# Two layers of hedgehog linear attention and squared-ReLU dense block: the join between dense layer and next keys, and the barrier at each layer's start, issued in another order

## The chip, the cores and the metric

One core of a Trainium2 chip runs the whole kernel. The metric is the device time of one execution in microseconds (us), and of the runs shown the median counts. The engines are TensorE (PE in the profile, its weight loads PEld), VectorE (DVE), ScalarE (ACT), GpSimd (POOL) and SyncE (SP, which issues most of the DMA transfers). Each engine works off its own queue in order.

## The reference

Input x has 2048 rows (S) of 576 features (D); there are 32 heads of 18 features and 4608 hidden features. Two layers, each with the same weights, are computed in float32:

```
x = x + A(layernorm(x));  x = x + B(layernorm(x))          # twice
A:  q, k, v = x @ wqkv
    phi(q) = [softmax(q @ w_phi), softmax(-q @ w_phi)]      # per head
    kv = phi(k)^T v ;  z = sum over rows of phi(k)
    o  = phi(q) kv / (phi(q) z + 1e-6) ;  return o @ wo
B:  return relu(x @ w1 + b1)^2 @ w2 + b2
```

Each layer's `kv` and `z` are sums over all rows, so no row can leave layer 1's attention before the last row has left layer 0's dense block.

## The kernel before

**Tiling.** Rows are cut into 4 blocks of 512 (`NB`), each of 4 tiles of 128 (`NT`). Features are held transposed in 5 chunks (four of 128 and a rest of 64), hidden features in 36 chunks `f` of 128 (`NF`). To keep float32 accuracy, each operand of a product is split into a high part that PE reads exactly and a low part that holds the rest, and a product is made of three: high by high, low by high, high by low. The split costs a copy (ACT) and a subtraction (DVE or POOL).

**Order.** A generator traces each stage's instructions; `weave` runs two of them against each other at a given rate, `pipeline` steps tiles through stages, and each `yield` gives the cost of the step. `chained` and `held` put what is traced behind the last instruction of each engine so that the scheduler, which builds the final queue of every engine, can't move it ahead. The blocks are taken as [3, 2, 0, 1]. Blocks 3 and 2 have a dense block each, 0 and 1 share one (`g_pair`): `products` does the first product of both and the second product of block 0, and `seconds` then does the second product of block 1, one `f` after the other, with 12 matmuls of 448 columns and 3 of 512 for each `f`. For a coming `f`, one SP transfer brings the weights (`m_pr`), another the squared activations (`m_pg`), and ACT, DVE and POOL split them into `m_ps` (L1190 to L1192) and `m_phc` (L1276).

**The join.** In layer 0, `seconds` is woven with `back_keys`, which makes layer 1's keys and values of blocks 3, 2 and 0 while PE still works on the dense chunks. For each block it norms four tiles (`n_3`, `n_2`, `n_0`), transposes them on PE in six steps (two pairs of tiles, and behind each pair its rests), splits the result (L412, L413), projects values (`v_3pv`, weights `w_3v0`, `w_3v1` for the two halves of the heads) and keys (`k_3kp`, weights `w_3k0`, `w_3k1`), turns keys into features (the `k_3K` tiles) and adds a tile's share to the sums `kvp`. The value and key weights take turns in the same buffers, and half 0 of the keys needs the buffer that half 0 of the values leaves. A tile's norm is mean and variance on DVE (L375, L376), a power on POOL (`n_2d`, L378) and two scalings on DVE (L393, L394). Block 0 has its keys alone here. Products and transposes share two PSUM buffers (`w`), so a third group can start on PE only when the first has been split.

**The barrier.** At the start of each layer (names `t0` and `t1`) the last blocks' values and sums are finished, the sums are turned into operands (`sums_operands`: `zb`, `ko`, `kbh`, `kbl`, and for the last four heads `kq` with the products `kt`, in `last_group`), and one block's query features are divided by their sums. This is `g_phi`: for tile t, two products `t0fm` (half on DVE, half on POOL), two sums and a few small steps on DVE, and the scaling of the features `t0fQ` by `t0fQr` (half on DVE, half on POOL). `g_out` then transposes the scaled features (L768, `t0opt`), multiplies them by the operands (`t0opn`) and by the output weights (`t0oo0`, `t0oo1`), first for tiles 0 and 1 (part 0) and then for tiles 2 and 3. In layer 0 the output weights are split here, with the low parts on POOL (L331); layer 1 loads the kept parts.

Of the kernel before, what the change touches and what calls it, by code (L numbers as in the profile page):

```python
# [7 lines left out]
F32 = mybir.dt.float32  # L8
# [5 lines left out]
P = 128  # L14
TB = 512
# [6 lines left out]
def layers_kernel(  # L22
# [322 lines left out]

    def moved(which, half, pair, back):
        for piece, home in zip(pair, wsplit[which]):
            for p, c0, c1 in parts_of(which):
                at = half * NC * HP
                here = piece[p, c0:c1].rearrange("p c n -> p (c n)").bitcast(F32)  # L350
                there = home[p, at + c0 * HP : at + c1 * HP]
                nc.sync.dma_start(*((there, here) if back else (here, there)))
# [28 lines left out]
    def g_norm(x_of, dst, name, then=None, fine=False):  # L381
# [3 lines left out]

        def scale(t):
            x = x_of(t)
            mv, rstd = moments(x, t, name)
            if fine:
# [50 lines left out]
        if not fine:  # L440
            yield from lagged(NT, scale, turn_all)
            return
        xns, pts = {}, {}

        def apart(t):
            xns[t] = scale(t)

# [38 lines left out]

    def make_v(x, t, pair, name):
        vt = vslots[dense["v"] % NT]
        dense["v"] += 1
        v3 = vt[:, : H * VW].rearrange("p (h d) -> p h d", d=VW)  # L490
        for half in range(2):
            pt = project(x, t, pair[half], f"{name}pv{half}{t}")
            dense["evicted"] = nc.scalar.activation(v3[:, half * H // 2 : (half + 1) * H // 2, 1:],
                                                    pt[:, :HP].rearrange("p (h d) -> p h d", d=DH), AF.Copy)
        return vt
# [83 lines left out]
    def sums_operands(layer):  # L579
# [22 lines left out]
        def keep(own, parts):  # L602
            hi, lo = parts
            nc.scalar.activation(hi, own, AF.Copy)
            nc.vector.tensor_sub(lo, own, hi.bitcast(F32))


        for s in range(2):
            pt = wtile(f"kt{layer}{s}")
# [11 lines left out]
        def last_group():  # L621
            w = gw[last]
            own = sb.tile([P, TB], F32, tag="hr", name=f"kq{layer}", bufs=2)
            own = own[:, : 2 * w].rearrange("p (s q f) -> p s q f", s=2, q=NQ)
            nc.vector.tensor_mul(own, kv[:, :, HG].unsqueeze(2).to_broadcast([P, 2, NQ, DH]),
                                 quarter.unsqueeze(1).unsqueeze(3).to_broadcast([P, 2, NQ, DH]))
            pt = wtile(f"kt{layer}2")
            p3 = pt[:w, : 2 * w].rearrange("p (s n) -> p s n", s=2)
            with tc.issue_after(dense["projected"].ins):
                for s in range(2):  # L630
                    nc.tensor.matmul(p3[:, s], own[:, s].rearrange("p q f -> p (q f)"),
                                     place.rearrange("p q d -> p (q d)"), start=True, stop=True)
            keep(p3, [k[:w, :, last, :w] for k in (kbh, kbl)])
# [75 lines left out]
    def phi_scale(e, r):  # L709
        for s in range(2):  # L710
            e3 = e[:, s].rearrange("p (h d) -> p h d", d=DH)
            (nc.gpsimd if s else nc.vector).tensor_mul(
                e3, e3, r[:, s].unsqueeze(2).to_broadcast([P, H, DH]))
# [29 lines left out]
    def g_out(layer, b, ph, dst, name, parts=1, pause=None, behind=None, norm=None, mid=None, costs=(None, None)):  # L743
# [377 lines left out]
    def g_pair(layer, blocks, x, after, name):  # L1121
# [217 lines left out]
        def seconds():  # L1339
# [21 lines left out]
    def g_attend(layer, b, x, raws, dst, name, behind=None, norm=None, mid=(None, None), ph=None):  # L1361
# [8 lines left out]
        if mid[0]:  # L1370
            yield from mid[0]
        yield from g_out(layer, b, ph, dst, name, behind=behind and behind["last"], norm=norm, mid=mid[1],
                         costs=(1.0, None if norm else 3.0))
# [10 lines left out]
    def barrier(layer, b, prev, x, xprev, kes, vpair):  # L1384
# [39 lines left out]
        drain(softs)  # L1424
        last_group = sums_operands(layer)
        spare["tags"] = [f"acc{i}" for i in range(NC)] + ["h"]
        phi = g_phi(layer, er, ph, f"{n}f")
        for _ in range(4):
            next(phi)
            next(queries)  # L1430
            next(queries, None)
        drain(queries)
# [38 lines left out]
    for layer in range(2):  # L1471
# [24 lines left out]
        def back_keys():  # L1496
            new_slots("vs")
            late = []
            for b in order[:3]:
                m = f"1_{b}"  # L1500
                last = b == order[2]
                xk, vts, raws, es, rs = {}, [], {}, {}, {}
                yield from g_norm(rows_of(b), xk, f"n{m}", fine=True)
                while late:
                    kv_tile(1, *late.pop(0))
                    yield 0.8
                if not last:
                    spill(b, xk)
                    yield from paced(g_v(xk, wpair("v", f"w{m}"), vts, f"v{m}"), 1.0)
                pair = wpair("k", f"w{m}")  # L1510

                def raw(t):
                    raws[t] = make_raw(xk, t, pair, f"k{m}k")

# [66 lines left out]
```

## Time and profile before

| what | value |
|---|---|
| runs | 2531.08, 2533.43, 2536.16 us (median 2533.43) |
| profiled execution | 2538.57 us, of which the span from first to last instruction is 2536.8 |
| mean granted PE clock | 0.992 |
| PE busy | 2481.7 us, 98% of the span |
| join and dense work around it, 1170 to 1345 us | PE busy 159.51 of 175 us, clock 0.95, DMA share 0.62 |
| barrier of layer 0, 195 to 250 us | PE busy 45.10 of 55 us, clock 0.94 |
| barrier of layer 1, 1455 to 1505 us | PE busy 45.08 of 50 us, clock 0.97 |

The last three rows are windows of the trace. An engine's row in the list of waits reads: the instruction that waited and its line, the instruction that it waited for and its line, the sum of the waits in us, how many, and the longest. A window reads: busy time of PE, PEld, DVE, ACT and POOL, then the granted clock of PE as a share of full speed, the share of DMA engines busy, and GB/s. A row of a timeline reads: start, duration, engine, line, operation, output and inputs, shapes, and in brackets the idle time ahead of it with what ended it.

### The profile page before, as it was taken

Reading aid. Unit: us, or ns where it says so; the run is one execution under the profiler, and the core shown is the slowest. Engines: PE = TensorE matmul, PEld = TensorE weight load, DVE = VectorE, ACT = ScalarE, POOL = GpSimd, SP = SyncE. Lnnn points to the kernel's source line nnn. Section 1 sums busy time; section 2 is a strip of 40 time slices with the busy share of each in tenths; the row PEclk is TensorE's granted clock in tenths of the full one; section 3 lists DMA queues with packets and bytes.
Section 4 is the critical chain, followed back from the end, with each engine's and each line's share of the span. In section 5 each row is a group of like instructions: output and inputs, shape, how many; then the busy total and the mean of one; then the engine's idle time right before and its main releaser. Section 6 shows DMA issues by size and latency. Waiting matters only on the chain.

```text
span 2536.8 us, 41468 instructions
## 1 busy us (share of the span) xinstructions
PE 2481.7 (98%) x15108; PEld 2179.8 (86%) x15108; DVE 1570.9 (62%) x2514; ACT 1265.5 (50%) x2245; POOL 949.5 (37%) x1101
## 2 busy tenths in 40 slices
PE   8998999999999999999999989999999999999999
PEld 8997888889888888888889988888898888888888
DVE  6778848554856655554667679394548566555444
ACT  4344545443446666663333435454445466666642
POOL 3544312212325555551333333031123355565322
PEclk8999999999999999999999999999999999999999
DMA  9222643356434433328654134333563444333363
GB/s 326 79 69 91 196 116 85 103 164 213 133 119 125 143 114 99 113 93 295 206 180 148 47 128 150 102 99 98 166 222 112 129 130 142 116 96 109 112 199 127
DMA packets 249691, 348.52 MB, mean 137 GB/s; under 512 B 30158, under 2 KB 157262, under 8 KB 246926
## 3 DMA queue, kind: packets, MB, share of 16 engines
q1 hardware_dynamic: 248228, 343.18, 42.7%
q8 instruction: 118, 1.93, 0.3%
q10 hardware_dynamic: 1258, 2.70, 0.3%
q14 instruction: 87, 0.71, 0.1%
HBM read 279.46 MB, written 66.32 MB: 136 GB/s over the span
## 4 chain that ended last, share of the span: by engine, by line
PE 47%; DVE 3%; DMA 2%; ACT 1%; POOL 1%; issue 1%; SPq 0%; DVEq 0%; ACTq 0%; POOLq 0%
PE m_1ph L887 5%; PE m_0ph L887 4%; PE m_pacacc L1231 4%; PE m_ppx L1202 4%; PE m_1acc L914 3%; PE m_0acc L914 3%; PE m_pacc L1231 3%; PE m_ppy L1202 2%; PE m_pacacc L1221 2%; PE m_pach L1231 1%; PE m_0acc L905 1%; PE m_1acc L905 1%; PE m_pacc L1221 1%; PE m_ppz L1202 1%; PE a_0po L805 1%
## 5 line engine op out<-in xcount | busy, mean ns | idle before, releaser
L1192 POOL TENSOR_TENSOR m_ps<-m_pr,m_ps 128x128 fp32r<-128x128 f32 x144 | 118.2, 821 | 338.6 <-ACT m_ps L1190 282.9
L1191 DVE TENSOR_TENSOR m_ps<-m_pr,m_ps 128x448 fp32r<-128x448 f32 x144 | 98.1, 681 | 194.7 <-ACT m_ps L1190 191.3
L1231 PE MATMUL m_pacc<-m_ps,m_phb 128*128 128x448 f32 x864 | 188.5, 366 | 0.0
L1231 PEld LDWEIGHTS m_pacc<-m_ps,m_phb 128*128 128x128 f32 x864 | 162.2, 188 | 18.0
L1190 ACT ACTIVATE m_ps<-m_pr 128x576 fp32r<-128x576 f32 x144 | 98.1, 681 | 154.5 <-issue 88.2
L1231 PE MATMUL m_pacacc<-m_ps,m_phc 128*128 128x448 f32 x648 | 147.7, 370 | 0.0
L1231 PEld LDWEIGHTS m_pacacc<-m_ps,m_phc 128*128 128x128 f32 x648 | 122.6, 190 | 9.9
L1212 DVE TENSOR_TENSOR m_phb<-m_pz,m_phb 128x512 fp32r<-128x512 f32 x72 | 56.5, 784 | 113.1 <-ACT m_pz L1211 111.6
L914 PE MATMUL m_2acc<-m_2s,m_2hb 128*128 128x448 f32 x432 | 100.2, 366 | 0.0
L914 PE MATMUL m_0acc<-m_0s,m_0hb 128*128 128x448 f32 x432 | 100.1, 366 | 0.0
L887 PE MATMUL m_3ph<-t0onh,m_3h 128*128 128x512 f32 (+1 forms) x380 | 98.0, 383 | 1.6 <-DVE t0onh L426 0.8
L914 PE MATMUL m_1acc<-m_1s,m_1hb 128*128 128x448 f32 x432 | 99.4, 365 | 0.0
L914 PE MATMUL m_3acc<-m_3s,m_3hb 128*128 128x448 f32 x432 | 99.4, 365 | 0.0
L887 PE MATMUL m_1ph<-t1onh,m_1h 128*128 128x512 f32 (+1 forms) x380 | 97.8, 382 | 1.5 <-DVE t1onh L426 0.8
L887 PE MATMUL m_0ph<-a_0nh,m_0h 128*128 128x512 f32 (+1 forms) x380 | 97.8, 384 | 0.0
L887 PE MATMUL m_2ph<-a_2nh,m_2h 128*128 128x512 f32 (+1 forms) x380 | 97.8, 384 | 0.0
L914 PEld LDWEIGHTS m_2acc<-m_2s,m_2hb 128*128 128x128 f32 x432 | 80.9, 188 | 10.5 <-ACT m_2hb L895 0.2
L914 PEld LDWEIGHTS m_0acc<-m_0s,m_0hb 128*128 128x128 f32 x432 | 80.9, 188 | 10.6 <-ACT m_0hb L895 0.2
L914 PEld LDWEIGHTS m_1acc<-m_1s,m_1hb 128*128 128x128 f32 x432 | 81.1, 188 | 10.3
L914 PEld LDWEIGHTS m_3acc<-m_3s,m_3hb 128*128 128x128 f32 x432 | 81.1, 188 | 10.3
L872 POOL TENSOR_TENSOR m_3s<-m_3r,m_3s 128x128 fp32r<-128x128 f32 x36 | 24.6, 683 | 168.6 <-ACT m_3s L867 154.1
L872 POOL TENSOR_TENSOR m_1s<-m_1r,m_1s 128x128 fp32r<-128x128 f32 x36 | 24.7, 686 | 167.7 <-ACT m_1s L867 153.3
(2440 smaller groups left out, 7372.1 us busy)
## 6 DMA issues: line engine op xcount, KB each, us to landing
m_pr<-in_B_w SPq DMA_DIRECT2D x144, 288.0 KB
m_pr<-in_B_w SPq DMA_DIRECT2D x72, 256.0 KB
hd<-m_pu SPq DMA_DIRECT2D x72, 256.0 KB
m_pg<-hd SPq DMA_DIRECT2D x72, 256.0 KB
m_3r<-in_B_w SPq DMA_DIRECT2D x36, 288.0 KB
m_2r<-in_B_w SPq DMA_DIRECT2D x36, 288.0 KB
m_1r<-in_B_w SPq DMA_DIRECT2D x36, 288.0 KB
m_0r<-in_B_w SPq DMA_DIRECT2D x36, 288.0 KB
```

Of the source, the lines that this page charges most:

```text
L805: nc.tensor.matmul(pt[:, :HP], a, m[:w, g], start=(g == 0 and k == 0), stop=(g == NG - 1 and k == 2))
L872: nc.gpsimd.tensor_sub(s2[:, D + R : 2 * D], r2[:, R:], s2[:, R:D].bitcast(F32))
L887: dense["hidden"] = nc.tensor.matmul(ph[:, cols], a, m, start=(k == 0), stop=(k == len(ops) - 1))
L905: nc.tensor.matmul(acc[KC], a, m, start=(f == 0 and k == 0), stop=(f == NF - 1 and k == 2))
L914: nc.tensor.matmul(acc[t][:, :R], a[:, rows], m, start=(f == 0 and k == 0), stop=(f == NF - 1 and k == 2))
L1190: nc.scalar.activation(s2[:, :D], r2, AF.Copy)
L1191: nc.vector.tensor_sub(s2[:, D : D + R], r2[:, :R], s2[:, :R].bitcast(F32))
L1192: nc.gpsimd.tensor_sub(s2[:, D + R : 2 * D], r2[:, R:], s2[:, R:D].bitcast(F32))
L1202: nc.tensor.matmul(ps, a, m, start=start and i == 0, stop=i == len(ms) - 1, skip_group_check=True)
L1212: nc.vector.tensor_sub(hl, r, hh.bitcast(F32))
L1221: nc.tensor.matmul(accs[b][KC], a, m, start=(g == 0 and k == 0), stop=(g == NF - 1 and k == 2))
L1231: nc.tensor.matmul(accs[b][t][:, :R], a[:, rows], m, start=(g == 0 and k == 0), stop=(g == NF - 1 and k == 2))
```

## The change

Part 1 is the join. `chained` gets a strict form which also puts each step of `back_keys` behind PE's last traced instruction. `seconds` yields five times in each `f` instead of once, and the rate goes from 4.0 to 0.85; six instead of two steps are taken within the last paired product. The norm is cut into statistics and scaling, pipelined over tiles, and the first six steps of the next block's norm (tiles 0 to 2) run between the value products of the block before. Values are made by halves: half 0 for all four tiles, then half 1. Key weights load half by half when the value half is done (`g_load`), value weights during the norm.

Part 2 is the barrier of both layers. `kq` is made ahead of the `ko` and `kbl` work; the third tile's products and sums (the fifth step of `phi`) are no longer run ahead of `g_out` and so come in its drain behind part 0; the output weights' pieces are issued behind `kbh` and behind POOL's scaling of tile 1, in place of the last eviction.

```diff
-    def chained(gen):
+    def chained(gen, strict=False):
...
+            if strict:
+                ends[nc.tensor.engine] = traced_on(nc.tensor)
...
+    def g_load(which, half, name, into):
+        into[half] = piece_tiles(f"{name}{which}{half}", TAGS_A)
+        for p in range(2):
+            with tc.issue_after(traced_on(nc.sync)):
+                moved(which, half, into[half], False, (p,))
+            yield 1.0
...
-        for t in range(NT):
-            apart(t)
-            yield 2.2
-        yield from pipeline(3 * NT // 2, (cross, split), (0.3, 0.6))
+        yield from pipeline(NT, (start, apart), (2.0, 1.6))
+        yield from pipeline(3 * NT // 2, (cross, split), (0.3, 0.9))
...
-            nc.scalar.activation(hi, own, AF.Copy)
+            dense["kbh"] = nc.scalar.activation(hi, own, AF.Copy)
...
+        kq = sb.tile([P, KC * P], F32, tag="xn", name=f"kq{layer}")
...
-            with tc.issue_after(behind.ins) if behind else nullcontext():
+            with ExitStack() as order:
+                for ins in behind or ():
+                    order.enter_context(tc.issue_after(ins.ins))
...
-                second(f)
+                for t in range(NT):
+                    by_rows(f, [t], range(3))
+                    yield
+                features(f, range(3))
+                del high[f], wide[f]
...
         last_group()
-        next(phi)
         dst = {}
-        drain(g_out(layer, b, ph, dst, f"{n}o", 2, phi, dense["evicted"]))
+        drain(g_out(layer, b, ph, dst, f"{n}o", 2, phi, (kbh, scaled)))
...
-                    yield from paced(g_v(xk, wpair("v", f"w{m}"), vts, f"v{m}"), 1.0)
-                pair = wpair("k", f"w{m}")
+                    norm = norm_of(order[i + 1])
+                    vts = [next_slot() for _ in range(NT)]
+                    for half in range(2):
+                        for t in range(NT):
+                            half_v(xk, t, wv[half], half, vts[t], f"v{m}")
+                            yield 0.5
+                            if len(ahead) < 6:
+                                ahead.append(t)
+                                yield next(norm)
+                        yield from paced(g_load("k", half, f"w{m}", wk), 0.3)
...
-                                    (1.0, 2.6, 0.4, 1.8, 0.8))
+                                    (0.5, 2.4, 0.4, 2.0, 0.8))
...
-        back = iter(()) if layer else chained(back_keys())
+        back = iter(()) if layer else chained(back_keys(), True)
         for k, _ in enumerate(products):
             if k == NP - 1:
-                next(back, None)
-                next(back, None)
-        weave(seconds, back, 4.0)
+                for _ in range(6):
+                    next(back, None)
+        weave(seconds, back, 0.85)
```

Three places show what moves. The first is DVE's queue in the join between block 3's last key features and the first splits of block 2's transposes, before the change (`n_2s` statistics, `n_2n` scaling, `n_2l` split; `m_ps` and `m_phc` are dense operands):

```order
L375 BN_STATS n_2s_12822<-x_2_1_12820 128x6 x2
L376 BN_AGGR n_2m_12823<-n_2s_12822 128x2
L393 TENSOR_SCALAR n_2n_12830<-x_2_1_12820,n_2m_12823,n_2d_12824 128x512
L394 TENSOR_SCALAR n_2e<-x_2_1_12820,n_2m_12823,n_2d_12824 128x128
L375 BN_STATS n_2s_12861<-x_2_2_12859 128x6 x2
L1191 TENSOR_TENSOR m_ps_50_12835<-m_pr_50_12833,m_ps_50_12835 128x448
L1276 TENSOR_TENSOR m_phc_12841<-m_pg_12839,m_phc_12841 128x512
L376 BN_AGGR n_2m_12862<-n_2s_12861 128x2
L393 TENSOR_SCALAR n_2n_12869<-x_2_2_12859,n_2m_12862,n_2d_12863 128x512
```

And now, in the same place:

```order
L558 RECIPROCAL k_3K3r<-k_3K3r 128x64
L1218 TENSOR_TENSOR m_ps_50_12779<-m_pr_50_12777,m_ps_50_12779 128x448
L1303 TENSOR_TENSOR m_phc_12785<-m_pg_12783,m_phc_12785 128x512
L389 BN_STATS n_2s_12891<-x_2_3_12889 128x6 x2
L390 BN_AGGR n_2m_12892<-n_2s_12891 128x2
L410 TENSOR_SCALAR n_2n_12905<-x_2_3_12889,n_2m_12892,n_2d_12893 128x512
L411 TENSOR_SCALAR n_2e<-x_2_3_12889,n_2m_12892,n_2d_12893 128x128
L1218 TENSOR_TENSOR m_ps_51_12842<-m_pr_51_12840,m_ps_51_12842 128x448
L1303 TENSOR_TENSOR m_phc_12848<-m_pg_12846,m_phc_12848 128x512
L1218 TENSOR_TENSOR m_ps_52_12913<-m_pr_52_12911,m_ps_52_12913 128x448
L1303 TENSOR_TENSOR m_phc_12919<-m_pg_12917,m_phc_12919 128x512
L430 TENSOR_TENSOR n_2l<-n_2p_12925,n_2h 128x4x128
```

Only tile 3's norm is left there; tiles 0 to 2 stand further up, among block 3's value products. On PE, the dense work ahead of the third group of transposes (`n_2e`) is one `f` shorter than before.

The second is PE's queue where block 3's values end and its keys begin, as it is now (L1258 and L1248 are dense matmuls, `w_3v1` and `w_3k1` the second halves of value and key weights):

```order
L502 MATMUL v_3pv_12438<-w_3v1h,n_3h 128x288 x5
L502 MATMUL v_3pv_12438<-w_3v1h,n_3l 128x288 x4
L502 MATMUL v_3pv_12438<-w_3v1l,n_3h 128x288 x5
L1258 MATMUL m_pacacc_12010<-m_ps_42_12216,m_phc_12222 128x448 x3
L502 MATMUL k_3kp_12462<-w_3k0h,n_3h 128x288 x5
L502 MATMUL k_3kp_12462<-w_3k0h,n_3l 128x288 x4
L502 MATMUL k_3kp_12462<-w_3k0l,n_3h 128x288 x5
L1258 MATMUL m_pacacc_12011<-m_ps_42_12216,m_phc_12222 128x448 x3
L1248 MATMUL m_pacacc_12012<-m_phc_12222,m_ps_42_12216 128x512 x3
L1258 MATMUL m_pach<-m_ps_43_12287,m_phc_12293 128x448 x2
L502 MATMUL k_3kp_12478<-w_3k1h,n_3h 128x288 x5
```

The transfer of `w_3k1` can begin behind the first three rows, whose buffer it takes, and its first use is the last row. Before, both key halves were loaded together while the last value products ran.

The third is POOL's queue in layer 0's barrier. Before (`t0oo0l` and `t0oo1l` are the low parts, `m_3s` and `m_3h` dense weights' low parts):

```order
L331 TENSOR_TENSOR t0oo0l<-t0oo0r,t0oo0h 126x1152
L331 TENSOR_TENSOR t0oo0l<-t0oo0r,t0oo0h 72x288
L331 TENSOR_TENSOR t0oo1l<-t0oo1r,t0oo1h 126x1152
L694 TENSOR_TENSOR t0fm_2836<-t0fQ0e,zb_2802 128x576
L331 TENSOR_TENSOR t0oo1l<-t0oo1r,t0oo1h 72x288
L694 TENSOR_TENSOR t0fm_2913<-t0fQ1e,zb_2802 128x576
L712 TENSOR_TENSOR t0fQ0e<-t0fQ0e,t0fQ0r 128x576
L694 TENSOR_TENSOR t0fm_2981<-t0fQ2e,zb_2802 128x576
L712 TENSOR_TENSOR t0fQ1e<-t0fQ1e,t0fQ1r 128x576
L872 TENSOR_TENSOR m_3s_0_3482<-m_3r_0_3476,m_3s_0_3482 128x128
```

And now:

```order
L719 TENSOR_TENSOR t0fm_2915<-t0fQ1e,zb_2802 128x576
L737 TENSOR_TENSOR t0fQ0e<-t0fQ0e,t0fQ0r 128x576
L737 TENSOR_TENSOR t0fQ1e<-t0fQ1e,t0fQ1r 128x576
L336 TENSOR_TENSOR t0oo0l<-t0oo0r,t0oo0h 126x1152
L336 TENSOR_TENSOR t0oo0l<-t0oo0r,t0oo0h 72x288
L336 TENSOR_TENSOR t0oo1l<-t0oo1r,t0oo1h 126x1152
L336 TENSOR_TENSOR t0oo1l<-t0oo1r,t0oo1h 72x288
L895 TENSOR_TENSOR m_3h_0_3481<-m_3r_0_3475,m_3h_0_3481 128x640
L899 TENSOR_TENSOR m_3s_0_3482<-m_3r_0_3476,m_3s_0_3482 128x128
L899 TENSOR_TENSOR m_3s_1_3508<-m_3r_1_3502,m_3s_1_3508 128x128
L895 TENSOR_TENSOR m_3h_1_3507<-m_3r_1_3501,m_3h_1_3507 128x640
L719 TENSOR_TENSOR t0fm_3115<-t0fQ2e,zb_2802 128x576
```

The low parts now stand behind the scaling of tiles 0 and 1, and the third tile's product (`t0fm` of `t0fQ2e`) behind them and the dense weights.

More of the change, by code (lines that the diff above doesn't have):

```diff
@@ L344, in parts_of, with moved @@
         return [(slice(0, P), 0, NC)]
-    def moved(which, half, pair, back):
-        for piece, home in zip(pair, wsplit[which]):
+    def moved(which, half, pair, back, only=(0, 1)):
+        for i in only:
+            piece, home = pair[i], wsplit[which][i]
             for p, c0, c1 in parts_of(which):
@@ L622, in last_group @@
             w = gw[last]
[L623 to L626, printed above, removed]
             pt = wtile(f"kt{layer}2")
@@ L1371, in g_attend @@
             yield from mid[0]
-        yield from g_out(layer, b, ph, dst, name, behind=behind and behind["last"], norm=norm, mid=mid[1],
+        yield from g_out(layer, b, ph, dst, name, behind=behind and (behind["last"],), norm=norm, mid=mid[1],
                          costs=(1.0, None if norm else 3.0))
@@ L1425, in barrier @@
         last_group = sums_operands(layer)
+        kbh = dense["kbh"]
         spare["tags"] = [f"acc{i}" for i in range(NC)] + ["h"]
@@ L1497, in back_keys, with norm_of @@
             new_slots("vs")
-            late = []
-            for b in order[:3]:
+            late, ahead = [], []
+            normed = {b: {} for b in order[:3]}
+            def norm_of(b):
+                return g_norm(rows_of(b), normed[b], f"n1_{b}", fine=True)
+            norm = norm_of(order[0])
+            for i, b in enumerate(order[:3]):
                 m = f"1_{b}"
                 last = b == order[2]
-                xk, vts, raws, es, rs = {}, [], {}, {}, {}
-                yield from g_norm(rows_of(b), xk, f"n{m}", fine=True)
+                xk, vts, raws, es, rs = normed[b], [], {}, {}, {}
+                wv, wk = {}, {}
+                which, ready = ("k", wk) if last else ("v", wv)
+                loads = (cost for half in range(2) for cost in g_load(which, half, f"w{m}", ready))
+                for n, cost in enumerate(norm):
+                    yield cost
+                    if n > 5:
+                        next(loads, None)
+                drain(loads)
                 while late:
```

38 lines of the change are left out of this document (27 added, 11 removed).

## The prediction, made before the change was run

> **What bounds the kernel now.** I read the busy line of the page first, then the waits of TensorE (PE), then its clock by windows, then the timelines around the waits.
>
> ```profile
> PE 2481.7 (98%) x15108; PEld 2179.8 (86%) x15108; DVE 1570.9 (62%) x2514; ACT 1265.5 (50%) x2245; POOL 949.5 (37%) x1101
> ```
>
> PE sets the time; the other engines have slack on average. The change adds and removes no product of weight, so it can gain only what PE idles, some 55 us of the 2536.8 us span, and what the clock loses behind idle stretches. The waits (engine, line waited for, total, times, longest):
>
> ```profile
> PE n_2p L418 <- DVE n_2l L413: 6.1, 1, 6.1
> PE n_0p L418 <- DVE n_0l L413: 5.6, 1, 5.6
> PE t0opt L768 <- DVE t0fQ1e L712: 3.5, 1, 3.5
> ...
> PE kt L631 <- DVE kq L625: 2.2, 1, 2.2
> PE t1opt L768 <- DVE t1fQ1e L712: 2.0, 1, 2.0
> PE k_3kp L484 <- DMA w_3k0h<-wskh: 1.9, 1, 1.9
> PE n_3p L418 <- DVE n_3l L413: 1.8, 1, 1.8
> ...
> PE t0opt L768 <- DVE t0fQ0e L712: 1.2, 1, 1.2
> ...
> PE t1opt L768 <- DVE t1fQ3e L712: 0.9, 1, 0.9
> PE t0opt L768 <- DVE t0fQ3e L712: 0.9, 1, 0.9
> ```
>
> Four are in the join (n_2p, n_0p, k_3kp, n_3p: 15.4 us), three at the start of layer 0's barrier (kt and t0opt: 6.9 us), one in layer 1's (2.0). The windows give the clock behind them (PEclk, third number from the right):
>
> ```profile
> 1195.00:1200.00 5.00, 3.14 (x16) 2.68 (x16) 0.00 (x0) 0.41 (x1) 0.00 (x0) 0.93 1.01 370
> 1200.00:1205.00 5.00, 5.00 (x23) 4.56 (x23) 1.13 (x2) 1.50 (x3) 0.90 (x1) 0.72 0.48 198
> 1250.00:1255.00 5.00, 2.09 (x7) 1.91 (x8) 4.45 (x9) 0.38 (x1) 0.38 (x1) 0.55 0.68 222
> 1255.00:1260.00 5.00, 4.96 (x83) 3.96 (x82) 2.04 (x4) 2.38 (x5) 0.90 (x1) 0.76 0.24 73
> 1330.00:1335.00 5.00, 2.62 (x8) 2.41 (x9) 4.91 (x9) 0.90 (x2) 1.12 (x3) 0.50 0.71 211
> 1335.00:1340.00 5.00, 5.00 (x88) 3.97 (x88) 2.32 (x5) 2.55 (x5) 0.32 (x1) 0.91 0.41 125
> 215.00:220.00 5.00, 1.14 (x5) 0.98 (x6) 4.98 (x8) 0.35 (x2) 4.10 (x4) 0.63 0.00 0
> 220.00:225.00 5.00, 5.00 (x34) 5.00 (x32) 3.41 (x9) 3.22 (x10) 4.21 (x4) 0.69 0.37 107
> 1475.00:1480.00 5.00, 5.00 (x33) 5.00 (x31) 3.57 (x11) 3.06 (x10) 4.52 (x4) 0.66 0.32 93
> 1490.00:1495.00 5.00, 4.08 (x33) 3.85 (x34) 4.34 (x11) 3.19 (x10) 0.21 (x1) 1.00 0.00 0
> ```
>
> PE's busy time times the missing clock is the extra price of a wait: 3.14 x 0.07 + 5.00 x 0.28 = 1.6 us behind the key load's wait, 2.1 behind n_2p, 1.8 behind n_0p, 2.0 in the first barrier, 1.7 in the second. The 0.9 us wait for t1fQ3e left the clock at 1.00. So the join holds 15.4 + 5.5 = 20.9 us, barrier 0 6.9 + 2.0 = 8.9, barrier 1 2.0 + 1.7 = 3.7. The page "TensorE: Matmul & The Clock Gate" of the Trainium skill (section "Why this matters for your kernels") asks only that no idle gap exceed about 3 us; the trace differs, with clock 0.72 behind a wait of 1.9 us, so the measurement is used. By the page, the two waits of 1.9 and 2.0 us would carry no clock price and the gain below would be about 3 us smaller, inside the range.
>
> **The join's two long waits.** The third pair of transposes needs a PSUM buffer that the vector engine (DVE) frees by a split (L413), and that split stands in DVE's queue behind the norm of all four tiles:
>
> ```profile
> 1240.71 0.81 DVE L375 BATCH_NORM_STATS2 n_2s<-x 128x6 f32<-128x288 f32 x2
> ...
> 1244.33 0.60 DVE L1191 TENSOR_TENSOR m_ps<-m_pr,m_ps 128x448 fp32r<-128x448 f32 x1
> ...
> 1250.38 0.61 DVE L1191 TENSOR_TENSOR m_ps<-m_pr,m_ps 128x448 fp32r<-128x448 f32 x1
> ...
> 1252.16 1.29 DVE L413 TENSOR_TENSOR n_2l<-n_2p,n_2h 128x512 fp32r<-128x512 f32 x2
> ```
>
> From 1240.71 to 1250.38 are three tiles' norms, 9.7 us with 1.2 us of dense splits among them: 8.5 us. After the change three of four tiles are normed under the previous block's value products, where DVE was wholly idle (0.00 busy in 1195 to 1200), so the split comes 8.5 us earlier. PE comes earlier too, since the order puts about 3 us less dense work (one f) ahead of the transposes. 6.1 + 3 - 8.5 = 0.6, and 0.1 at n_0p: of both waits I leave 0.5 us, without a clock price (the 0.9 us wait had none). Bounds: nothing left, or 2 us each with 2 us of clock, if DVE's dense splits fall next to more POOL work. The 1.8 us of n_3p I count as gone: transposes now stand apart by dense row pieces, and the 0.9 instead of 0.6 step gives DVE room. The six steps instead of two in the last paired product cost nothing: they pull loads and norms under PE work. The finer yields and the rate 0.85 (4.25 steps' worth per f against 4.0) move only the place of PE's work; cover: 6 f's of dense work remain behind the last transposes' keys. Without it 3.1 us per missing f.
>
> **Key weights.** Half 0 of block 3's keys now loads when value half 0 is done, one value half earlier than PE needs it, at least four half-products of 1.9 us; its 1.9 us wait goes. Half 1 can be issued only behind the last value product, since it takes that buffer.
>
> ```profile
> 1192.64 0.32 SPq L352 DMA_DIRECT2D w_3k0h<-wskh  x1
> ...
> 1198.99 1.24 PE L484 MATMUL k_3kp<-w_3k0h,n_3h 128*128 128x288 f32 x5 [1.86 <-DMA w_3k0h<-wskh]
> ...
> 1215.91 0.78 PE L1231 MATMUL m_pach<-m_ps,m_phc 128*128 128x448 f32 x3
> ...
> 1222.15 0.82 PE L484 MATMUL k_3kp<-w_3k0h,n_3h 128*128 128x288 f32 x5
> ...
> 1225.86 0.36 PE L1231 MATMUL m_pach<-m_ps,m_phc 128*128 128x448 f32 x1
> ```
>
> From issue to use the trace shows 6.35 us with other loads queued. Between the last value product and the first product with half 1 the new order has 14 key products (half of the tile that took 1222.15 to 1225.86: 1.9 us) and 8 of 12 narrow plus all three wide dense products (two f's took 1215.91 to 1222.15, 3.1 each: 2.3): 4.2 us. Late by 0 to 2.15 us in blocks 3 and 2 each. With less queued ahead (half 0 is long there) I take 1.0 each, 2.0 together, near the middle and below the clock's price. The other new loads (value weights in the norm, row tiles ahead) lie tens of us ahead of use. **Join: -20.9 + 1.0 + 2.0 = -17.9 us** (bounds -20.9 and -9).
>
> **Barrier, layer 0.** The low parts of the output weights run on GpSimd (POOL) beside DVE's `kbl`:
>
> ```profile
> 198.04 3.94 POOL L331 TENSOR_TENSOR t0oo0l<-t0oo0r,t0oo0h 126x1152 fp32r<-126x1152 f32 x2 [4.82 <-ACT t0oo0h L330]
> 201.95 2.67 POOL L331 TENSOR_TENSOR t0oo1l<-t0oo1r,t0oo1h 126x1152 fp32r<-126x1152 f32 x1
> ```
>
> ```profile
> 201.38 7.77 DVE L605 TENSOR_TENSOR kbl<-ko,kbh 126x504 fp32r<-126x504 f32 x2
> ...
> 215.36 1.69 DVE L694 TENSOR_TENSOR t0fm<-t0fQ2e,zb 128x576 f32<-128x576 f32 x1
> ...
> 217.10 0.74 DVE L700 TENSOR_REDUCE t0fu<-t0fm 128x32 f32<-128x576 f32 x1
> ...
> 228.00 0.42 DVE L788 TENSOR_TENSOR t0oolt<-t0opn,t0ooh 72x256 fp32r<-72x256 f32 x1 [0.82 <-ACT t0ooh L786]
> ```
>
> ```profile
> 1462.01 2.37 DVE L605 TENSOR_TENSOR kbl<-ko,kbh 126x504 fp32r<-126x504 f32 x2
> ```
>
> The same pair took 2.37 us in layer 1, where no low parts run: 5.4 us. DVE's chain to the second tile's scaling also loses the third tile's product and first sum (1.69 + 0.74) and kq (about 0.3, moved early into idle time): 8.1 us against 6.9 us of waits, so all three go, with their clock: -8.9. The rule in the Trainium skill that bears on it ("SBUF — State Buffer", section "SBUF: two separate sides") makes the port pair shared by DVE and GpSimd an exclusive lock, in both directions, for DVE operations with two SBUF inputs; 7.77 against 2.37 agrees. By it the moved low parts are not free either: a later DVE product of that kind waits out the POOL operation under way (2.67 us for the longest), and the gain would be up to 2.7 us smaller.
>
> What comes back: the third tile's product and two sums now stand behind DVE's `t0oolt` (end 228.42), 0.7 + 2 x 0.7 = 2.1 us more before the wait for t0fQ3e. And POOL is behind:
>
> ```profile
> 217.32 1.16 POOL L712 TENSOR_TENSOR t0fQ1e<-t0fQ1e,t0fQ1r 128x576 f32<-128x576 f32 x1 [0.90 <-DVE t0fQ1r L707]
> ...
> 222.79 1.43 POOL L694 TENSOR_TENSOR t0fm<-t0fQ3e,zb 128x576 f32<-128x576 f32 x1
> ```
>
> On the old clock POOL ends the scaling at 218.48, then the low parts (3.94 + 2.67 = 6.6), the dense weights' low parts between these rows (4.3), the third tile's product (1.43): 230.8, less 1.2 by which DVE's chain gains on PE, 229.6; DVE wants it at 229.1. Late by 0.5, up to 2.5 with blocking; I take 1.5. The wait grows by 3.6 and then costs clock like the first did (2.0). **Barrier 0: -8.9 + 3.6 + 2.0 = -3.3** (bounds -6.8 and +2). **Layer 1:** 3.7 go, 2.1 come back at t1fQ3e (POOL is in time, no low parts), and a wait of 3.0 costs a clock price like 1.7: **+0.1** (bounds -2 and +1).
>
> **Sum:** -17.9 - 3.3 + 0.1 = -21.1 us. Against the profiled execution, 2538.57 us (span 2536.8 and 1.8 around it), 2517.5. That execution was 5.1 above the median 2533.43, just above the runs' 2531.08 to 2536.16; taken off the median: **2512.3 us**.
>
> **Rivals.** *Key half 1 late* in both blocks by the full 2.15 us, each with 1.6 of clock: 7.5 in place of 2.0, 2517.8 us. For it: the load starts behind the last value product. Against: less is queued than in the row above. Chance 0.13. *The barriers give back more:* `kbl` still beside a POOL product (2 us of waits stay), and POOL late by 4.5 instead of 1.5 us, since the moved low parts now meet DVE's later products: 2517.3. Chance 0.10. *The waits only move:* the norm ahead of time doesn't shorten DVE's queue at the split because its rows arrive late, and PE, 3 us earlier, waits 9 us twice: +16 against the join's 17.9, near 2528 to 2532. For it, DVE is 4.45 and 4.91 of 5 busy around those waits; against, DVE's empty value stage. Chance 0.11. *Slower:* in the value stage the half-products share two PSUM buffers, freed by ScalarE (ACT), whose queue now holds dense copies between every two evictions. If each of the 16 half-products waited over (21.1 + 5)/16 = 1.6 us for its buffer, the time would pass 2538.5; at 2 us each, 2544. Against: in 1195 to 1200 ACT is busy 0.41 of 5 us, and no value product is among the waits. Chance 0.10.
>
> **Numbers.** Forecast 0.56. A measurement of this kernel tells about 0.2% (5 us) from none: faster 0.56 + 0.13 + 0.10 = 0.79, same 0.11, slower 0.10. Range: 2506 (the join's and barriers' better bounds mostly reached) to 2527 (join at -9, barriers as in the second rival, or the waits half moved).
>
> **What would show it.** Right: no wait at n_2p and n_0p above 1 us and clock 0.95 or more in the join; `kbl` in layer 0 near 2.4 us; waits for t0fQ3e near 4.5 and t1fQ3e near 3 us, with a clock dip behind. Wrong: a wait for w_3k1h or w_2k1h over 2 us, value products or dense products waiting for ACT or DVE in the join, or the t0opt waits for t0fQ1e still there.

## The result, and the profile after

The changed kernel took 2520.09 us (median of 4 runs, 2517.87 to 2522.35) against 2532.37 us for the kernel before (4 runs beside them, 2531.08 to 2536.16): 12.3 us less, a ratio of 0.9948 with a 95% interval of 0.9932 to 0.9964. A second comparison gave 0.9949 [0.9936, 0.9963]. The time lies in the predicted range, but the gain is little more than half of the 21.1 us that the prediction summed. The span of the profiled execution, on the other hand, fell by 20.7 us, from 2536.8 to 2516.1: nearly the predicted sum. Most of this study is about that difference.

First the busy line of the page of the changed kernel:

```profile
PE 2474.3 (98%) x15108; PEld 2171.1 (86%) x15108; DVE 1560.9 (62%) x2514; ACT 1265.5 (50%) x2245; POOL 949.2 (38%) x1101
```

PE idles 41.8 us of the span where it idled 55.1, and is busy 7.4 us less with the same 15108 matmuls. PE's busy time times the missing clock, added up over windows of 5 us, is 15.7 us in the profile of before and 6.1 in this one, so the clock is enough to account for that part. Then the list of PE's waits (line numbers are up to 27 higher than before):

```profile
PE t0opt L793 <- DVE t0fQ2e L737: 4.2, 1, 4.2
...
PE m_pacc L1248 <- DVE m_phb L1239: 1.7, 1, 1.7
...
PE n_0p L435 <- DVE n_0l L430: 1.6, 1, 1.6
PE k_3kp L502 <- DMA w_3k1h<-wskh: 1.5, 1, 1.5
PE t1opt L793 <- POOL t1fQ3e L737: 1.1, 1, 1.1
...
PE t0opt L793 <- POOL t0fQ3e L737: 0.6, 1, 0.6
...
PE t1opt L793 <- DVE t1fQ2e L737: 0.4, 1, 0.4
PE n_2p L435 <- DVE n_2l L430: 0.3, 1, 0.3
```

Of the join's four waits (15.4 us) n_2p has 0.3 and n_0p 1.6 left, and half 1 of the keys (1.5) and a dense operand (m_phb, 1.7) have come: 5.1 in all. In layer 0's barrier the waits for kq, t0fQ0e and t0fQ1e are gone, and the later wait is 4.8 us in place of 0.9. Its cause stands in DVE's timeline (start, duration, line, operation):

```profile
200.43 2.52 DVE L630 TENSOR_TENSOR kbl<-ko,kbh 126x504 fp32r<-126x504 f32 x2
...
218.52 0.42 DVE L813 TENSOR_TENSOR t0oolt<-t0opn,t0ooh 72x256 fp32r<-72x256 f32 x1 [0.82 <-ACT t0ooh L811]
218.86 4.54 DVE L719 TENSOR_TENSOR t0fm<-t0fQ2e,zb 128x576 f32<-128x576 f32 x1
223.33 1.40 DVE L725 TENSOR_REDUCE t0fu<-t0fm 128x32 f32<-128x576 f32 x2
```

and in POOL's, over the same time:

```profile
210.71 3.41 POOL L336 TENSOR_TENSOR t0oo0l<-t0oo0r,t0oo0h 126x1152 fp32r<-126x1152 f32 x2
214.09 3.44 POOL L336 TENSOR_TENSOR t0oo1l<-t0oo1r,t0oo1h 126x1152 fp32r<-126x1152 f32 x2
217.47 1.57 POOL L895 TENSOR_TENSOR m_3h<-m_3r,m_3h 128x640 fp32r<-128x640 f32 x1
219.00 0.88 POOL L899 TENSOR_TENSOR m_3s<-m_3r,m_3s 128x128 fp32r<-128x128 f32 x2
219.84 1.57 POOL L895 TENSOR_TENSOR m_3h<-m_3r,m_3h 128x640 fp32r<-128x640 f32 x1
221.37 1.42 POOL L719 TENSOR_TENSOR t0fm<-t0fQ2e,zb 128x576 f32<-128x576 f32 x1
222.75 1.95 POOL L719 TENSOR_TENSOR t0fm<-t0fQ3e,zb 128x576 f32<-128x576 f32 x1
```

`kbl` takes 2.52 us where it took 7.77, as the low parts no longer run beside it. But the third tile's product on DVE, which takes 0.74 us in layer 1, now takes 4.54, the time until POOL has worked off the dense weights' low parts and its own half of that product. The stall has moved to the next DVE operation of that kind.

**Where the time went, stretch by stretch.** The starts of five kinds of PE's instructions cut the program at the same places in each kernel. Three profiles of the kernel before (two of them taken as experiments below) and two of the changed one give, in us:

| stretch | before | change | mean difference | predicted |
|---|---|---|---|---|
| start to the first value product of barrier 0 (t0pv) | 158.9, 156.3, 158.1 | 158.5, 157.3 | +0.1 | 0 |
| barrier 0: t0pv to the first dense product (m_3ph) | 95.5, 96.0, 95.9 | 93.4, 94.3 | -1.9 | -3.3 |
| dense blocks and join: m_3ph to t1pv | 1166.9, 1163.6, 1164.0 | 1149.6, 1153.7 | -13.2 | -17.9 |
| barrier 1: t1pv to m_1ph | 88.0, 86.5, 86.6 | 86.6, 86.7 | -0.4 | +0.1 |
| m_1ph to the end | 1027.5, 1027.4, 1027.9 | 1028.0, 1031.0 | +1.9 | 0 |
| span | 2536.8, 2529.8, 2532.5 | 2516.1, 2523.0 | -13.5 | -21.1 |

With more than one profile of each the difference is 13.5 us, close to that of the medians. The first profile of before was the longest and the first of the change the shortest, and that pair alone said 20.7. In the stretch with the join, 9.2 of the 13.2 us are idle time of PE (19.0 us on average before, 9.8 now) and 4.0 are busy time. In barrier 0 PE idles 2.8 us less and is busy 0.9 us more.

### The profile page after: what moved, and what is told of

Read it like the earlier page. It is cut to its first block, busy times and chain, and to the rows that moved or that the text cites. A ratio compares the mean times of both kernels' runs of the same rounds, so it can differ in the third digit from the quotient of the medians.

```text
span 2516.1 us, 41454 instructions
## 1 busy us (share of the span) xinstructions
PE 2474.3 (98%) x15108; PEld 2171.1 (86%) x15108; DVE 1560.9 (62%) x2514; ACT 1265.5 (50%) x2245; POOL 949.2 (38%) x1101
## 4 chain that ended last, share of the span: by engine, by line
PE 90%; DVE 4%; DMA 2%; ACT 2%; POOL 1%; issue 1%; SPq 1%; DVEq 0%; ACTq 0%; POOLq 0%
PE m_ppx L1229 8%; PE m_pacc L1258 6%; PE m_pacacc L1258 5%; PE m_1ph L914 5%; PE m_3ph L914 5%; PE m_2ph L914 5%; PE m_0ph L914 4%; PE m_ppy L1229 4%; PE m_2acc L941 3%; PE m_1acc L941 3%; PE m_0acc L941 3%; PE m_3acc L941 3%; PE m_pacacc L1248 2%; PE m_ppz L1229 2%; PE m_pacc L1248 2%; PE m_pach L1258 2%
## 5 line engine op out<-in xcount | busy, mean ns | idle before, releaser
L1258 PE MATMUL m_pacc<-m_ps,m_phb 128*128 128x448 f32 x864 | 188.4, 366 | 0.0
L1258 PEld LDWEIGHTS m_pacc<-m_ps,m_phb 128*128 128x128 f32 x864 | 162.2, 188 | 17.9
L1258 PE MATMUL m_pacacc<-m_ps,m_phc 128*128 128x448 f32 x648 | 149.2, 368 | 0.0
L1258 PEld LDWEIGHTS m_pacacc<-m_ps,m_phc 128*128 128x128 f32 x648 | 119.4, 188 | 9.1
```

The lines of the kernel that those rows point to most:

```text
L1258: nc.tensor.matmul(accs[b][t][:, :R], a[:, rows], m, start=(g == 0 and k == 0), stop=(g == NF - 1 and k == 2))
```

## The experiments

Twelve runs were made in three comparisons; three of them repeat the change or the kernel before for a further profile. The median of before was 2532.27, 2532.15 and 2532.02 us in the three.

**1. The change again** (no edit).

> The changed kernel again, to see what its gain is made of. Its profiled execution was 20.7 us shorter in span than that of before (idle of TensorE 13.3 us less, busy 7.4 less, which is clock), its median only 12.3 us. Theory A (the clock price behind a wait varies from execution to execution, and the profile of before was an execution with much of it): executions of before have spans near 2529 to 2531 us at clocks of 0.994 to 0.996, and at equal clock the two kernels stand 12 to 14 us apart, the idle removed. Theory B (the clock price is part of every such wait): the executions of before have the clock 0.992 of its profile, and the kernels stand 18 to 21 us apart.

2520.82 us (5 runs, 2516.97 to 2524.68). Thirteen of the 15 executions of before had clocks of 0.993 to 0.995, with spans of 2528.6 to 2533.6; two had 0.992 like the profile on which the prediction was built (2532.3 and 2536.1). This execution of the change had a span of 2523.0, 6.9 us longer than the first: PE idled 2.2 us more and was busy 4.7 us more (2479.0). The two kernels' medians stand 11.5 us apart, a little under theory A's range; B's 18 to 21 is excluded by the interval (9.4 to 16.2 us). Over all the profiles of the two kernels PE's idle time fell by 11.3 us on average and its busy time by 2.2, so the gain is mostly, but not only, idle time.

**2. Two further profiles of before** (no edit).

> The kernel of before once more, for another profile. Theory A (the clock price behind a wait is a draw of each execution): the waits of the join are the same to 0.3 us (6.1, 5.6, 1.8, 0.7 to 1.9), while TensorE's busy time times the missing clock, 5.7 us in the join's windows of the first profile, comes out between 2 and 6, and between 1 and 7 in the first 150 us. Theory B (fixed price): within 0.5 us of 5.7 in the join.

> The same kernel of before, a further profile, with the same expectations: theory A, join 2 to 6 us of missing clock and not that of the profile before it; theory B, 5.2 to 6.2.

2531.56 and 2534.26 us. For each profile I multiplied PE's busy time by the missing clock in every window of 5 us and added up four stretches (0 to 150, 195 to 250, 1150 to 1345, 1400 to 1510 us):

| profile | first 150 us | barrier 0 | join | barrier 1 |
|---|---|---|---|---|
| before, first | 6.3 | 2.0 | 5.7 | 1.7 |
| before, second | 1.7 | 2.8 | 4.9 | 0.0 |
| before, third | 3.9 | 3.0 | 4.3 | 0.0 |
| change, first | 3.2 | 2.9 | 0.0 | 0.0 |
| change, second | 4.5 | 3.5 | 1.4 | 0.0 |
| barrier alone (4) | 1.7 | 2.7 | 4.4 | 1.6 |
| dense low parts late (7) | 1.6 | 0.0 | 0.0 | 1.6 |

Theory B's bounds for the join (5.2 to 6.2) fail, but A's "2 to 6" was too wide. Behind the two long waits, n_2p and n_0p together, the three profiles of before lost 4.1, 4.9 and 4.3 us and that of experiment 4 lost 4.4: waits of 5 to 6 us cost clock each time, and nearly the same. The rest of the 5.7 is what stood behind the key load's wait in the first profile alone. Waits of about 2 us cost clock in some executions and not in others, so theory A holds for these alone. In barrier 1 of before the same wait of 2.0 us cost 1.7 us once and nothing twice. The key load's wait behind which the prediction read a clock of 0.72 was 1.4 us in the second profile, with no cost (windows of that profile: busy times, then clock, DMA share, GB/s):

```profile
1190.00:1195.00 5.00, 3.60 (x22) 3.14 (x22) 0.00 (x0) 0.41 (x1) 0.00 (x0) 1.00 1.04 388
1195.00:1200.00 5.00, 5.00 (x32) 4.74 (x31) 1.49 (x2) 1.50 (x3) 0.90 (x1) 1.00 0.67 246
...
1245.00:1250.00 5.00, 3.29 (x10) 2.93 (x11) 3.25 (x6) 0.38 (x1) 0.00 (x0) 0.55 0.83 276
1250.00:1255.00 5.00, 5.00 (x85) 4.25 (x84) 3.03 (x5) 2.78 (x5) 0.90 (x1) 0.76 0.27 73
```

The first two rows stand around the key load's wait, the last two behind n_2p. The n_3p wait of 1.8 us was absent in both further profiles of before, against theory A's "the same to 0.3 us", the key load's was 1.4 and 1.0, and the second of the two has a wait of 0.7 us for m_phb: the join idled 13.0 and 13.4 us there, not 15.4.

**3. The join alone.** The barrier's edits are taken back:

```diff
-        drain(g_out(layer, b, ph, dst, f"{n}o", 2, phi, (kbh, scaled)))
+        next(phi)
+        drain(g_out(layer, b, ph, dst, f"{n}o", 2, phi, (dense["evicted"],)))
```

(and kq is again made in `last_group`).

> The join of the change with the barrier of before. If the gain is the join's idle (15.4 us of waits down to 3.4 in the profile): 10 to 12 us faster than before. If the clock price went with it each time, as the prediction summed: 17 to 18 us faster. Waits in layer 0's barrier are back: kt near 2.2, t0fQ1e near 3.5.

2520.61 us, ratio 0.9952 [0.9940, 0.9965]: 11.7 us less than before, as much as the whole change. The waits for kq (2.2), t0fQ1e (3.4) and t1fQ1e (2.0) are back. The 17 to 18 us of a fixed clock price lie outside the interval. That is not because the clock of the long waits stayed: this profile lost none in the join, where those of before lost 4.3 to 5.7. The join had less idle time to lose than 15.4 us, and 4.6 us of waits are left in it, not 3.4 (1.6 for w_3k1h, 1.5 at n_0p, 1.2 for m_phb, 0.3 at n_2p).

**4. The barrier alone**, with the join of before (the diff's part 2 on the kernel before).

> The barrier of the change with the join of before. The prediction's -3.3 and +0.1: about 3 us faster. From the profiles' waits alone (7.8 us of waits in layer 0 down to 4.8, 2.9 down to 1.7 in layer 1): 3 to 4 us faster without clock. Rival: the barrier gives back all that it takes, within 1.5 us of before, since the wait of 4.2 us for t0fQ2e is long enough to cost clock where the three before were shorter each.

2531.74 us, ratio 0.9997 [0.9988, 1.0006]. The rival holds: nothing that can be measured is left, though 3 us less is just at the interval's edge. Of PE's waits there:

```profile
PE n_2p L418 <- DVE n_2l L413: 6.1, 1, 6.1
PE n_0p L418 <- DVE n_0l L413: 5.5, 1, 5.5
PE t0opt L768 <- DVE t0fQ2e L712: 4.1, 1, 4.1
```

The join's two are untouched, and the new wait for t0fQ2e stands in the place of the three removed; its stretch is 93.9 us against 95.5 to 96.0.

**5. The third tile's sums early again.** One line is put back into the change:

```diff
         last_group()
+        next(phi)
         dst = {}
```

> The change with the third tile's product and sums back ahead of the transposes (the fifth step of phi), all else as changed, so the low parts stand behind the third tile's product on GpSimd. Theory: the 4.2 us wait for t0fQ2e came from the third tile's DVE product standing 4.5 us beside GpSimd's work; with it ahead that wait falls below 1.5 us, while the second tile's scaling comes about 2.4 us later and brings a wait of 0 to 1.5 us for t0fQ1e: 2 to 3 us faster than the change, and layer 1 within 1 us. Rival (the prediction's chain: the early sums are on the path to t0fQ1e): a wait of over 2 us for t0fQ1e comes back in both layers and the time is that of the change or longer.

2518.06 us, ratio 0.9941 [0.9929, 0.9954], which overlaps that of the change (0.9949): no difference is shown. Waits of 2.1 us for t0fQ1e and 2.3 for t1fQ1e came back, as the rival said. The theory was right that the wait for t0fQ2e goes, and the third tile's product takes 0.75 us on DVE. But the fourth tile's product now stands beside POOL's work and takes 2.00, and a wait of 3.2 us for t0fQ3e came. Moving the sums trades one wait for another in both layers.

**6. The dense stage in coarse steps.**

```diff
-                for t in range(NT):
-                    by_rows(f, [t], range(3))
-                    yield
-                features(f, range(3))
-                del high[f], wide[f]
+                second(f)
                 yield
...
-        weave(seconds, back, 0.85)
+        weave(seconds, back, 4.25)
```

> The change with the dense stage yielding once for each f again (rate 4.25 in place of 0.85 times five); norms ahead, value halves and the strict chain stay. Theory (the early norm is what removes the long waits): n_2p and n_0p wait below 2 us each, the time within 3 us of the change. Rival (the fine weave does it, by spreading transposes and giving DVE room between them): waits of 2 us or more come back at n_3p, n_2p or n_0p, and the time is 4 us or more longer than the change.

2518.73 us, ratio 0.9945 [0.9933, 0.9958]: within 3 us of the change. No wait over 0.5 us at n_3p, n_2p or n_0p; w_3k1h is waited for 1.7 us (1.5 and 2.0 in the change) and w_2k1h 1.2 (none and 0.6). The fine yields are not what removes the long waits.

**7. The dense weights' low parts late.** In the first two chunks of the dense block behind each barrier, POOL's subtractions are put behind its scaling of the last tile (shown for the first of two):

```diff
-            (nc.gpsimd if early else nc.vector).tensor_sub(l1, r1, h1.bitcast(F32))
+            with tc.issue_after(dense["scaled1"].ins) if early else nullcontext():
+                (nc.gpsimd if early else nc.vector).tensor_sub(l1, r1, h1.bitcast(F32))
```

> The change with GpSimd's low parts of the dense block's first two chunks (m_3h, m_3s; m_1h, m_1s in layer 1) behind its scaling of the last tile, where they stand ahead of the third tile's product in the change. Theory (the 4.2 us wait for t0fQ2e is GpSimd's queue, whose operations hold DVE's third product off): that product on DVE takes below 2 us in place of 4.5, the waits for t0fQ2e and t0fQ3e together fall from 4.8 to 2 us or less, and the time is 2 to 4 us below the change. Rival (the two sums behind t0oolt cost it, as in the prediction's 2.1): the waits stay above 3 us.

2511.54 us (5 runs, 2510.59 to 2513.32), ratio 0.9919 [0.9905, 0.9933]: 20.6 us less than before, and the fastest kernel of this study. DVE's timeline:

```profile
216.09 0.42 DVE L813 TENSOR_TENSOR t0oolt<-t0opn,t0ooh 72x256 fp32r<-72x256 f32 x1 [0.83 <-ACT t0ooh L811]
216.43 0.74 DVE L719 TENSOR_TENSOR t0fm<-t0fQ2e,zb 128x576 f32<-128x576 f32 x1
217.09 1.40 DVE L725 TENSOR_REDUCE t0fu<-t0fm 128x32 f32<-128x576 f32 x2
```

and POOL's:

```profile
215.02 1.42 POOL L719 TENSOR_TENSOR t0fm<-t0fQ2e,zb 128x576 f32<-128x576 f32 x1
216.40 2.07 POOL L719 TENSOR_TENSOR t0fm<-t0fQ3e,zb 128x576 f32<-128x576 f32 x1
...
225.14 3.58 POOL L896 TENSOR_TENSOR m_3h<-m_3r,m_3h 128x640 fp32r<-128x640 f32 x2
```

PE's waits for the scaled features of barrier 0 are now these:

```profile
PE t0opt L793 <- POOL t0fQ3e L737: 1.1, 1, 1.1
...
PE t0opt L793 <- DVE t0fQ2e L737: 0.4, 1, 0.4
...
PE t0opt L793 <- DVE t0fQ3e L737: 0.2, 1, 0.2
```

The product takes 0.74 us in place of 4.54, and the waits fall from 4.8 us to 1.7. The two sums are not what costs the time: they stand where they stood in the change. The stretch of barrier 0 is 88.1 us against 93.4 and 94.3 for the change, 5.8 us less: 3.1 of idle time and 2.7 of busy time, since this execution lost no clock there. The medians stand 9 us apart, more than the 2 to 4 expected and more than that stretch; the other stretches of its profile are within 3.4 us of the change's, and I can't say which of that repeats.

**8. The norm late again.** The steps of the next norm between the value products are left out, all else as in the change:

```diff
                             yield 0.5
-                            if len(ahead) < 6:
-                                ahead.append(t)
-                                yield next(norm)
```

> The change without the steps of the next block's norm between the value products: the norm runs whole behind the keys as before; fine yields, strict chain, value halves and loads stay. Theory (the early norm takes 8.5 us of DVE's work away from the splits): waits of 4 us or more at n_2p and at n_0p come back, 8 to 14 us with their clock, and the time is 8 to 14 us longer than the change, near 2528 to 2534. Rival (pipelined norm and fine weave are enough): both waits below 2 us, time within 3 us of the change.

2531.15 us (10 runs), ratio 0.9998 [0.9988, 1.0008]. Its waits:

```profile
PE n_0p L435 <- DVE n_0l L430: 4.2, 1, 4.2
PE t0opt L793 <- DVE t0fQ2e L737: 4.2, 1, 4.2
PE n_2p L435 <- DVE n_2l L430: 4.1, 1, 4.1
```

The theory holds: with this one edit undone both waits come back at over 4 us, a wait of 2.0 us for w_2k1h with them, and no gain is left in the time. The stretch from m_3ph to t1pv is 1160.5 us, 8.8 more than the change's mean: by this profile the early norms are 8.8 of the 13.2 us that the change took off it. The two waits are shorter than before (6.1 and 5.6). Which of the other edits does that was not run: the strict order, the halves of the values and the key loads by halves were never taken back alone.

**9. The output weights' low parts as before**, beside kbl:

```diff
-        drain(g_out(layer, b, ph, dst, f"{n}o", 2, phi, (kbh, scaled)))
+        drain(g_out(layer, b, ph, dst, f"{n}o", 2, phi, (dense["evicted"],)))
```

> The change with the output weights' pieces issued behind the last eviction as before, so that in layer 0 GpSimd's low parts run beside DVE's kbl again. Theory (DVE is held off while GpSimd works): kbl takes over 6 us in place of 2.5, the wait for t0fQ1e is 2 to 4 us again, while the wait for t0fQ2e and t0fQ3e falls below 2.5, since GpSimd's queue is short there; layer 1 unchanged. In all within 3 us of the change. Rival (kbl's length in the first profile was chance): kbl near 2.5 us, and the time 2 us or more below the change.

2520.98 us, ratio 0.9958 [0.9943, 0.9973]: as the change. DVE's timeline shows the old length again, and the later product short:

```profile
199.38 7.78 DVE L630 TENSOR_TENSOR kbl<-ko,kbh 126x504 fp32r<-126x504 f32 x2
...
224.17 0.74 DVE L719 TENSOR_TENSOR t0fm<-t0fQ2e,zb 128x576 f32<-128x576 f32 x1
```

So 7.8 against 2.5 us is decided by what POOL does beside it, and no chance. The waits are 2.5 us for t0fQ0e and 1.8 for t0fQ1e (the expectation had 2 to 4 for the second alone) and 1.5 later: 5.8, against 4.8 in the change.

**10. Two steps in place of six** in the last paired product, on the kernel of 7 (`range(2)` for `range(6)`).

> The kernel with GpSimd's dense low parts behind the last scaling (2511.5 us), and two steps of the back in the last paired product in place of six. Theory (the six steps put three tiles' norm on DVE ahead of the dense operand m_phb): the wait of 0.7 to 1.8 us for m_phb is below 0.7, and what the steps gained at n_3p comes back as a wait of 0 to 2 us; time within 2 us of 2511.5. Rival: the steps feed the norm of the first block in time, and with two a wait of over 2 us comes at n_3p or at the first value product, 2513.5 or more.

2514.10 us, ratio 0.9929 [0.9916, 0.9941]. The wait for m_phb is gone, as is that at n_0p, and 0.8 us at n_3p came; but w_3k1h is waited for 2.6 us in place of 0.8. The time is 2.6 us above 2511.5, past the theory's 2 and on the rival's side, but without the wait of over 2 us that the rival named. No gain; the interval overlaps that of 7.

**11. Coarse steps on the kernel of 7.**

> The same kernel (2511.5 us) with the dense stage yielding once for each f. The change with that edit was 2518.7 against 2520.8 for the change: no wait at n_0p, but 1.2 us for w_2k1h. Expected if the two edits add: 2509.5 to 2512. Rival: the fine yields matter once the barrier's wait is gone, 2513.5 or more.

2516.36 us (2513.11 to 2518.43), ratio 0.9933 [0.9921, 0.9946], on the rival's side of 2513.5. Waits of 1.8 us for m_phb, 1.1 for w_3k1h and 2.0 for w_2k1h stand in its profile. Together with experiment 6, where the same edit cost nothing, this is not conclusive.

## Why the prediction was right or wrong

The direction, the range and the large mechanisms were right; the size was not. 21.1 us were summed and 12.3 measured.

- **The long waits of the join** were left 0.5 us each and have 0.3 and 1.6. Their cause was named rightly: experiment 8 brings them back with the norm alone.
- **Half 1 of the keys** was put at 2.0 us for both blocks; it is 1.5 in the first profile of the change and 2.0 + 0.6 in the second.
- **"The six steps cost nothing"** failed. DVE waits for a row tile's transfer and norms it ahead of the dense operand m_phb, and PE waits 1.7 us for that (with two steps, in experiment 10, it does not):

```profile
1153.15 0.82 DVE L389 BATCH_NORM_STATS2 n_3s<-x 128x6 f32<-128x288 f32 x2 [1.83 <-DMA x<-xs]
...
1156.07 0.68 DVE L1239 TENSOR_TENSOR m_phb<-m_pz,m_phb 128x512 fp32r<-128x512 f32 x1
```

- **The join's sum**, -17.9: the stretch fell by 13.2. It had less to lose (13.0 and 13.4 us of waits in the other two executions, for 15.4; clock 4.9 and 4.3, for 5.5) and got back more (5.1 and 6.3 us of waits in the two profiles, for 3.0, and 1.4 of clock behind m_phb in the second).
- **Barrier 0**, -3.3: the stretch fell by 1.9. That kbl shortens (2.37 forecast, 2.52 measured), that all three waits go, and that a later one grows to some 4.5 us (4.8) was right. POOL's lateness was taken as 1.5 us with up to 2.5 for blocking; DVE's product alone lost 3.8 us. The clock behind it was 2.9 and 3.5 for 2.0. The Trainium skill ("SBUF — State Buffer", section "SBUF: two separate sides") describes an exclusive lock between the two engines. The trace agrees, with 4.54 us beside POOL's work and 0.74 without. The prediction's own sentence on it was right about the place, the next DVE product with two operands in SBUF, and too low about the size: it had the product wait out one operation (up to 2.7 us), and it waited through five.
- **Barrier 1**, +0.1: -0.4. The wait came out at 0.4 + 1.1 + 0.2 us in place of 3.0; PE now transposes five pieces of t1fQ2e before it wants t1fQ3e, where the two took turns before. It cost no clock in either profile of the change, while the 1.7 us that were to go were there in one of three profiles of before.
- **The step that failed most** is the last: waits and clock prices were read off one execution, and their whole sum was taken off the median of the runs. That execution lay 5.1 us above the median, and much of its surplus stood in the very terms of the sum: 1.8 us at n_3p, 1.6 of clock behind the key load and 1.7 in barrier 1, none of which the two other profiles of before show. Its clock loss in the first 150 us was larger too (6.3, against 1.7 and 3.9). Set against its own profile the forecast was 2517.5, and the change's first profile took 2517.87; that is luck, since this was the fastest of four runs and the second profile took 2524.68. Why m_1ph to the end is 1.9 us longer in the change's two profiles stays open; one of them carries 1.5 us of clock there.

The rivals with the norm's waits only moving and with the value products waiting for their buffers are refuted: no value product waits in the change. Of the rivals' times, 2517.8 (key half 1) and 2517.3 (the barriers) lie nearest to the measured one. The first is not what happened: half 1 reaches 2.0 us in one block at most in the change, and no clock is lost behind it. The second is half right: the barriers gave back more than forecast, since a later DVE product waits out POOL's work, but kbl is short.

## What to carry to other kernels

Price a wait by its idle time, and take a clock price in full only behind waits of several microseconds; one behind a wait of 1 to 2 us is a draw, and one profile shows one draw. Before a sum goes from a profiled execution to a median, see by how much that execution is off and which of its terms are the surplus. When GpSimd work is moved away from one VectorE operation, look for the next one of the same kind in the queue: here the barrier's edit gained nothing until the dense weights' low parts were moved too, and then the kernel was 20.6 us faster than before rather than 12.3 (5.8 us of the profile's difference stand in that barrier).

## What the runs showed of the hardware

VectorE's held-off product did not get a turn between GpSimd's back-to-back operations. From 218.86 on, a product of 0.74 us waited through five of them (the row of `m_3s` holds two) and ended at 223.40 us, 0.65 us into a sixth, which took 1.95 us in place of 1.42. The same product took 4.51 us in the second profile of the change and in those of experiments 4 and 6.

The clock in the first 150 us, which no edit touches, cost between 1.7 and 6.3 us in three profiles of the kernel before, and nothing in that of experiment 10; all of it was lost between 10 and 40 us, around waits. The Trainium skill ("TensorE: Matmul & The Clock Gate", section "What's actually happening") says that the activity window runs freely, so that the start of one kernel is slow for a different number of matmuls from run to run. The traces agree in the first 10 us, where the windows' clock still reads 1.00: the same four transposes took 0.70 us in the first profile of before and 1.06 in the second, against 0.60 for such a group later. First profile:

```profile
7.90 0.70 PE L270 MATMUL fp<-ident,fr 128*126 128x128 f32 x4
```

Second profile:

```profile
7.96 1.06 PE L270 MATMUL fp<-ident,fr 128*126 128x128 f32 x4
```

In the middle of the program, too, the same wait costs a different amount from run to run; why is not shown. Waits of 0.4 us for t1fQ2e, then 1.1 and 0.2 for t1fQ3e, stand in nine profiles. They cost nothing in five, both profiles of the change among them, and 1.6 to 1.7 us in four. The windows around them in the first profile of the change:

```profile
1465.00:1470.00 5.00, 3.35 (x24) 2.62 (x22) 4.98 (x10) 0.00 (x0) 2.33 (x2) 1.00 0.35 113
1470.00:1475.00 5.00, 4.92 (x38) 4.31 (x37) 4.44 (x13) 4.22 (x13) 0.00 (x0) 1.00 0.00 0
```

and in the kernel of experiment 7:

```profile
1455.00:1460.00 5.00, 3.74 (x28) 3.27 (x26) 5.00 (x13) 0.00 (x0) 2.17 (x2) 1.00 0.52 172
1460.00:1465.00 5.00, 4.61 (x24) 4.19 (x24) 3.65 (x9) 2.40 (x8) 4.51 (x5) 0.66 0.22 64
```
